# Turning three more chunks with VectorE and DRAM instead of TensorE, with the tokens of turned chunks in another order

## Chip, cores and metric

The kernel runs on one core of a Trainium2 chip. The metric is the device time of one execution in microseconds, as the median over runs; the profile is one further execution that the hardware profiler recorded. Engines are named as in the profile: PE is TensorE (PEld its weight loads), DVE is VectorE, ACT is ScalarE, POOL is GpSimd, SP is SyncE, which issues the DMAs here.

## What is computed

Two transformer layers over 2048 tokens of width 448, each an attention with 16 heads of width 28 that share one key and one value head, and a gated feed-forward block of width 1792. Both layers use the same weights.

```python
def _A_ref(x, wq, wk, wv, wo):
    q = heads(x @ wq)                 # 16 heads, width 28
    k, v = x @ wk, x @ wv             # one head for all
    p = softmax(einsum("bhqd,bkd->bhqk", q, k) * 28 ** -0.5)
    return concat(einsum("bhqk,bkd->bhqd", p, v)) @ wo

def _B_ref(x, w_gate, w_up, w_down):
    return (silu(x @ w_gate) * (x @ w_up)) @ w_down

x = A_x                               # (1, 2048, 448)
for layer in range(2):
    x = x + _A_ref(layernorm(x), wq, wk, wv, wo)
    x = x + _B_ref(layernorm(x), w_gate, w_up, w_down)
```

## The kernel before

All products are taken in a split form: each fp32 operand is a high part and a low part (`xh`, `xl`), and three products of parts are added in PSUM. The tokens stand in four chunks of 512. A normalized chunk has its tokens on the partitions and must be turned, so that its 448 features stand on the partitions, before PE can multiply it by weights. There are two ways of turning:

- `flip` (L248): sixteen 128×128 transposes by PE into PSUM; then ACT casts the high part (L254) and DVE subtracts for the low part (L255, L264).
- `turn_tile` (L268, L271): DVE transposes a tile of 128 tokens in 32×32 blocks into `tb`, four stores (SP) put the blocks into their places in a DRAM tensor `xt`, in runs of 32 tokens (128 bytes); `rows3` (L130, L132) loads the whole turned chunk into an `xn` tile with three DMAs, and `halved` makes the two parts of it (casts L278, L282).

Before the change DVE turns only chunks 0 to 2 of the attention's output, in both layers, while the scores and softmax of later chunks run; everything else is flipped by PE, 160 transposes in all.

The feed-forward block works in units. A unit is one hidden tile `n` of a group `gi` (groups of `FG` = 2 tiles) for one chunk `c`. On PE a unit is: a first half of 11 pairs of products into two banks; the down projection of the unit before, part one; a second half of 10 pairs. Ahead of the parts that write a bank again, `between` (L325) lets ACT copy one column of each bank to `seen`, and PE waits for these copies. Then ACT takes Silu (L922), DVE the product (L923), ACT the high part (L924) and DVE the low part (L927) of the hidden tile. Down products of the unit go into the next one. With a chunk's last unit the residual `xres` gets its sum (`accumulate`: DVE L826; ACT L829 and POOL L830).

In the last group of layer 0 the next attention starts already. When a chunk's sum is done, which is in the unit after its last, `hand_over(c)` computes the statistics and orders the rest: `self.soon` is a list of steps that count down by one at the end of each unit, and run at zero; `self.mid` holds steps in the middle of a unit; `a.plan[n, 0]` and `a.plan[n, 1]` hold steps ahead of and behind projection `n`. `project` takes the next of the 16 projections (four rows of query/key/value per chunk); each copies its bank to a `stage` tile (L523, L524), stores it to `qd` and `kt` (L525, L528), and for two rows of a chunk turns the values on DVE and copies them on POOL (L531, L534). `maxima` (L424) takes the column maxima of a chunk at projections 6, 10 and 14; those of chunk 0 need the four query rows of chunk 0 back from DRAM (`fetch`, L444, with casts by POOL, L446).

Before the change the last group goes like this, with units as (c, n): chunk 0's normalization (L230) is at the end of (1,1), its flips in the middle of (2,0), two projections at the end of (2,0); chunk 1's normalization is at the end of (2,1), its flips in the middle of (3,0), one projection at the end of (3,0); chunk 2 is normalized at the end of (3,1) and flipped before projection 7; chunk 3's flips come before projection 11.

The order of instructions on each engine is the order in which the program issues them (`manual_schedule`); each engine works in order, so an instruction that waits holds up all that stands behind it on its engine. Tiles are laid out in pools in order of allocation; a tile that lies over an older one waits for the older one's last use. In the scores phase the pool `at` holds the buffers `pt0`, `single0`, ... of the exponentials (L614 to L619) and, in `turns`, `tb`.

Of the kernel before, what the change touches and what calls it, by code (L numbers as in the profile page):

```python
# [8 lines left out]
F32 = mybir.dt.float32  # L9
F32R = mybir.dt.float32r  # L10
# [5 lines left out]
P = 128  # L16
# [39 lines left out]
def forward(  # L56
# [54 lines left out]
    def bank(cands, hold=False):  # L111

        for _ in cands:
            turn[cands] = (turn.get(cands, -1) + 1) % len(cands)
            b = cands[turn[cands]]
            if b not in live:
                if hold:
                    live.add(b)
                return b, banks[b]
        raise AssertionError("no bank")  # L120
# [82 lines left out]
    def xtile(pool, again=None):  # L203

        return (
            pool.tile([P, 4, 512], F32R, name="xh"),
            pool.tile([P, 3, 512], F32R, name="xl"),
            again,
        )

    def norm_steps(c, pool=pers, twice=True):

        got = {}
        cs = slice(4 * c, 4 * c + 4)

        def stat(t):
            nc.vector.bn_stats(stats[:, 4 * c + t, :], xres[:, 4 * c + t, :])
            nc.vector.bn_aggr(mv[:, 4 * c + t, :], stats[:, 4 * c + t, :])

        def scale():  # L220
            rstd = pers.tile([P, 4], F32, name="rstd", bufs=2)
            nc.gpsimd.tensor_scalar(rstd, mv[:, cs, 1], 1.0, EPS, ALU.mult, ALU.add)
            nc.gpsimd.tensor_tensor(rstd, rstd, halfn, ALU.pow)
            got["r"] = rstd

        def apply(t):
            if t == 0:
                got["x"] = pool.tile([P, 4, 512], F32, name="xn")
            o, i, r = got["x"][:, t, 0:D], xres[:, 4 * c + t, :], got["r"][:, t : t + 1]
            nc.vector.tensor_scalar(o, i, mv[:, 4 * c + t, 0:1], r, ALU.subtract, ALU.mult)  # L230
            if twice:
                nc.gpsimd.tensor_copy(got["x"][:, t, D:512], o[:, 384:D])

        fs = [lambda t=t: stat(t) for t in range(4)] + [scale]
        return fs + [lambda t=t: apply(t) for t in range(4)], got
# [7 lines left out]
    def flip(got, tiles, ks=range(4), place=None):  # L243

        for k in ks:
            pt = place if place is not None else bank(wide[-1])[1]
            for t in range(4):
                nc.tensor.transpose(pt[:, P * t : P * t + P], got["x"][:, t, P * k : P * k + P], ident)  # L248
            flipped(tiles, k, pt, nc.vector.tensor_copy if place is not None else nc.scalar.copy)
# [13 lines left out]
            high = xd[64:128, :]  # L263
        nc.vector.tensor_tensor(xh[64:128, k, :], pt[64:128, :], high, ALU.subtract)  # L264

    def turn_tile(got, tb, raw, t):

        nc.vector.transpose(tb[:, t, :], got["x"][:, t, 0:D])  # L268
        to = raw.rearrange("(b d) (t g w) -> t g d b w", d=32, g=4, w=32)
        for g in range(4):  # L270
            nc.sync.dma_start(to[t, g], tb[32 * g : 32 * g + 32, t, :].rearrange("d (b w) -> d b w", w=32))  # L271

    def halved(tiles, r, ks, copy, sub):

# [54 lines left out]
    class Attention:  # L329


        def __init__(self, layer):
            self.layer = layer
            self.X, self.norms, self.qd = {}, {}, {}
            self.done = 0
            self.order = [(c, m) for c in range(NC) for m in (TURN if c < NC - 1 else LAST)]
            self.seen = 0
            self.steps, self.places = [], []
            self.lent, self.plan = None, {}
            self.hi, self.rowsof, self.kt, self.when = {}, {}, {}, {}  # L340
            for c in range(NC):
                self.kt[c] = dram.tile([32, 512], F32, name=f"kt{layer}_{c}")
                self.at(4 * c + 4, lambda c=c: self.key_load(c))
                self.at(4 * c + 7, lambda c=c: self.key_split(c))
            for i in range(3):
                self.at(4 + 3 * i, lambda i=i: self.stack(i))
                self.at(6 + 3 * i, lambda i=i: self.parts(i))
                if not full:
                    self.at((9, 11, 13)[i], lambda i=i: self.rows(i))
            if not full:  # L350
                self.at(2, self.first_keys)
                self.at(3, self.diagonal)
            for i in range(len(GR) if full else 0):
                fs, place = self.max_steps(i)
                if i == 1:
                    fs[KC] = lambda f=fs[KC]: (f(), self.places[0]())
                self.steps += fs
                self.places.append(place)
# [49 lines left out]
        def parts(self, i):  # L408
            q = qts[i % 3]
            split(q[:, 0, :], q[:, 1, :], qraw)  # L410
# [95 lines left out]

        def q(self, c, m):
            cs = slice(512 * c, 512 * c + 512)
            held, po = bank((3, 4, 5) if self.seen > len(self.order) - 4 else wide[-1], True)
            ms = slice(P * m, P * m + P)  # L510
            wh, wl = self.w
            product_T(po, [wh[:, k, ms] for k in range(4)], [wl[:, k, ms] for k in range(4)], self.X[c])
            if not full and self.seen in (6, 10, 14):
                self.maxima(self.seen // 4 - 1)
            live.remove(held)
            if c not in self.qd:
                self.qd[c] = dram.tile([D, 512], F32, name=f"qd{self.layer}_{c}")
            raw = self.pool.tile([P, 512], F32, name="stage")
            if not full and (c or not self.layer):
                if self.seen % 2 == 0:  # L520
                    self.two = wpool.tile([P, 2, 512], F32R, tag="wgh", name="q2", bufs=FG + 1)
                self.hi[m] = self.two[0:112, self.seen % 2, :]
                nc.scalar.copy(self.hi[m], po[0:112, :])  # L523
            nc.scalar.copy(raw, po)  # L524
            nc.sync.dma_start(self.qd[c][112 * m : 112 * m + 112, :], raw[0:112, :])  # L525
            d0, n = 16 * (m % 2), 12 if m % 2 else 16
            if m > 1:
                nc.sync.dma_start(self.kt[c][d0 : d0 + n, :], raw[112 : 112 + n, :])  # L528
                return
            vt = wpool.tile([P, 512], F32R, tag="wgl", name="vt", bufs=FG + 1).bitcast(F32)[96:128, :]  # L530
            nc.vector.transpose(vt, po[96:128, :])  # L531
            vt = vt.rearrange("p (t u d) -> p u t d", t=4, u=4)
            for u in range(4):
                nc.gpsimd.tensor_copy(  # L534
                    vsb[32 * u : 32 * u + 32, 4 * c : 4 * c + 4, d0 : d0 + n], vt[:, u, :, 16 : 16 + n]
                )
# [17 lines left out]
        def scores(self, ff, xb):  # L554
            next(switch)
            inner = ExitStack()
            with tc.tile_pool(name=f"ow{self.layer}", bufs=1, side="right", reuse_waits="tile") as ow:
                wp = inner.enter_context(tc.tile_pool(name=f"at{self.layer}", bufs=1, reuse_waits="tile"))
                woh = ow.tile([P, NG, D], F32R, name="woh")
                wol = ow.tile([P, NG, D], F32R, name="wol")  # L560
                on, accs, pts = {}, {}, {}
# [140 lines left out]

                def turns(c, got):

                    at_ = {}

                    def one(t):
                        if t == 0:
                            at_["tb"] = wp.tile([P, 4, D], F32, name="tb")
                        turn_tile(got, at_["tb"], ff.raw[c], t)  # L710

                    return [lambda t=t: one(t) for t in range(4)]

# [68 lines left out]
    class FeedForward:  # L782
# [61 lines left out]
        def hand_over(self, c):  # L844

            a = self.nxt
            fs, got = norm_steps(c)
            for f in fs[:5]:
                f()
            a.pool = self.stage  # L850
            a.X[c] = xtile((xpool, self.x1p, self.xbp, self.xbp)[c])

            def ready():
                for f in fs[5:]:
                    f()
                if c > 1:
                    a.norms[c] = got

            if c == NC - 1:
                a.plan[8, 0] = [ready]  # L860
                return
            self.soon.append([1, ready])
            if c < 2:
                self.mid[len(groups) - 1, c + 2, 0] = [lambda ks=ks: flip(got, a.X[c], ks) for ks in ((0, 1), (2, 3))]
                self.soon.append([2, lambda: [a.project() for _ in range(2 - c)]])

        def fetch(self, c):

# [19 lines left out]
        def unit(self, gi, c, n):  # L888
# [30 lines left out]
            two = halves("h2")  # L919
            hh, hl = two[:, 0, :], two[:, 1, :]  # L920
            sg = pers.tile([P, 512], F32, name="sg")
            nc.scalar.activation(sg, pg[0], AF.Silu)  # L922
            nc.vector.tensor_tensor(sg, pg[1], sg, ALU.mult)  # L923
            nc.scalar.copy(hh, sg)  # L924
            for f in first[:2]:
                f()
# [144 lines left out]
```

## Time and profile before

| | us |
|---|---|
| median of 3 runs | 1992.53 |
| lowest, highest run | 1992.45, 1994.26 |
| the profiled execution | 1995.44 |
| its span | 1993.7 |

The span is the stretch of the profiled execution from its first to its last recorded instruction. TensorE's granted clock was 0.997 of full speed.

| engine | busy us | share of the span |
|---|---|---|
| PE | 1973.1 | 99% |
| ACT | 1276.1 | 64% |
| DVE | 782.7 | 39% |
| POOL | 559.9 | 28% |

How to read rows of the profile: a group's row has the source line, the engine, the operation, output and input by the program's names, the shape of both, the count, then busy time in us, the mean of one in ns, and the idle time of the engine just before such instructions with what ended it. A row of the timeline has the start and the length in us, the engine (SPq is SP's queue, PEld weight loads), the line, the operation, and in brackets the idle time before it and what ended that. A row of the windows has a stretch of time and its length, the busy time of PE, PEld, DVE, ACT and POOL, each with the number of instructions, then the granted clock, the busy share of the DMA engines and GB/s. A row of the chain has the start and the length of a piece and what it was.

### The profile page before, as it was taken

How to read it: one execution, taken by the hardware profiler on the slowest of the kernel's cores; microseconds unless marked ns; L12 is line 12 of the kernel's file. 1: busy time of each engine (PE TensorE's matmuls, PEld its weight loads, DVE VectorE, ACT ScalarE, POOL GpSimd, SP SyncE). 2: the span in 40 equal slices, each digit the busy share in tenths (PEclk: the TensorE clock that was granted, in tenths of full speed). 3: DMA queues.
4: the chain of work that ended last, by engine and by line, in shares of the span. 5: the costliest groups of instructions: out<-in, count | busy, mean ns of one | idle time of the engine just before them, and what ended most of it. 6: DMA issues, size and time to landing. Idle time of an engine off the chain costs nothing.

```text
span 1993.7 us, 43630 instructions
## 1 busy us (share of the span) xinstructions
PE 1973.1 (99%) x18517; PEld 1305.8 (65%) x18517; DVE 782.7 (39%) x1370; ACT 1276.1 (64%) x2140; POOL 559.9 (28%) x611
## 2 busy tenths in 40 slices
PE   8999999999999999999999999999999999999998
PEld 7544534445458999999884444444454689988886
DVE  6443343443534232322464444435444432222222
ACT  4799798997963333333348997979979433333332
POOL 4213123122214233333341221132231243233320
PEclk9999999999999999999999999999999999999999
DMA  5201011021120111100031010200212200011102
GB/s 156 61 23 33 17 30 44 17 51 32 39 62 22 31 32 31 32 18 25 22 95 40 26 30 12 62 12 22 51 32 62 53 17 27 21 31 32 32 1 76
DMA packets 126496, 75.50 MB, mean 38 GB/s; under 512 B 69688, under 2 KB 110008, under 8 KB 126296
## 3 DMA queue, kind: packets, MB, share of 16 engines
q1 hardware_dynamic: 124744, 71.46, 13.5%
q8 instruction: 146, 2.39, 0.5%
q10 hardware_dynamic: 1552, 1.20, 0.2%
q14 instruction: 54, 0.44, 0.1%
HBM read 54.01 MB, written 17.83 MB: 36 GB/s over the span
## 4 chain that ended last, share of the span: by engine, by line
PE 96%; DVE 1%; DMA 1%; ACT 1%; POOL 0%; issue 0%; ACTq 0%; SPq 0%; DVEq 0%; POOLq 0%
PE bank L318 40%; PE bank L651 25%; PE three L592 20%; PE bank L298 4%; PE bank L592 3%; PE three L577 2%; PE bank L577 2%; PE bank L248 1%; DMA wr<-in_A_wq_dram 0%; DMA qd<-stage 0%; DVE xn L230 0%; DMA xd<-xh 0%; DMA kt<-stage 0%; DVE xres L581 0%; PE bank L424 0%
## 5 line engine op out<-in xcount | busy, mean ns | idle before, releaser
L651 PE MATMUL bank<-pt,vsb 128*32 128x512 f32 x3072 | 491.9, 600 | 0.0
L651 PE MATMUL bank<-single,vsb 128*32 128x512 f32 x1024 | 488.6, 600 | 0.0
L592 PE MATMUL bank<-qstack,keys 32*128 32x512 f32 x1536 | 470.5, 424 | 2.2 <-DVE xres L581 1.7
L592 PE MATMUL three<-qstack,keys 32*128 32x512 f32 x4608 | 461.7, 425 | 3.6 <-ACT pt L615 2.4
L318 PE MATMUL bank<-xh,wgh 64*128 64x512 f32 x1728 | 446.4, 389 | 0.0
L592 PEld LDWEIGHTS three<-qstack,keys 32*128 32x128 f32 x4608 | 251.6, 183 | 297.0 <-ACT pt L615 187.6
L618 ACT ACTIVATE pt<-three 128x1536 f32<-128x1536 f32 x256 | 408.7, 1597 | 0.0
L615 ACT ACTIVATE pt<-three 128x1536 f32<-128x1536 f32 x256 | 405.3, 1583 | 2.6 <-DMA kt<-stage 2.6
L318 PE MATMUL bank<-xh,wgl 64*128 64x512 f32 x1404 | 368.5, 390 | 0.0
L318 PE MATMUL bank<-xl,wgh 64*128 64x512 f32 x1296 | 334.7, 389 | 0.0
L318 PE MATMUL bank<-wdh,h 64*128 64x448 f32 x1792 | 332.5, 364 | 1.5 <-ACT h L924 0.8
L923 DVE TENSOR_TENSOR sg<-bank,sg 128x512 f32<-128x512 f32 x112 | 77.5, 692 | 507.6 <-ACT sg L922 503.5
L318 PEld LDWEIGHTS bank<-xh,wgh 64*128 64x128 f32 x1728 | 263.0, 184 | 18.1 <-issue 1.6
L651 PEld LDWEIGHTS bank<-pt,vsb 128*32 128x32 f32 x3072 | 101.9, 109 | 261.2 <-issue 153.3
L830 POOL TENSOR_TENSOR xres<-stage,xres 128x448 f32<-128x448 f32 x108 | 127.2, 1197 | 498.3 <-ACT stage L829 498.1
L660 DVE TENSOR_TENSOR o<-bank,o 128x512 f32<-128x512 f32 x224 | 154.9, 692 | 277.7 <-PE bank L651 277.7
L617 DVE COPY single<-bank 128x512 f32<-128x512 f32 x256 | 177.0, 691 | 211.4 <-PE bank L592 205.0
L318 PEld LDWEIGHTS bank<-wdh,h 64*128 64x128 f32 x1792 | 244.5, 184 | 16.0 <-issue 2.3
L694 POOL TENSOR_TENSOR o<-o 128x512 f32<-128x512 f32 x32 | 41.3, 1290 | 740.2 <-DMA o<-rd 331.6
L592 PEld LDWEIGHTS bank<-qstack,keys 32*128 32x128 f32 x1536 | 243.8, 183 | 5.4 <-DVE xres L581 3.6
L325 ACT COPY seen<-bank 128x1 f32<-128x1 f32 x664 | 81.9, 163 | 255.0 <-PE bank L318 252.3
L614 ACT ACTIVATE single<-bank 128x512 f32<-128x512 f32 x256 | 187.8, 734 | 64.4 <-PE bank L592 64.4
(131 smaller groups left out, 2716.8 us busy)
## 6 DMA issues: line engine op xcount, KB each, us to landing
o<-rd SPq DMA_DIRECT2D x32, 256.0 KB
qd<-stage SPq DMA_DIRECT2D x32, 224.0 KB
qraw<-qd SPq DMA_DIRECT2D x128, 56.0 KB
wdr<-in_B_w_down_dram SPq DMA_DIRECT2D x28, 224.0 KB
xt<-tb SPq DMA_DIRECT2D x96, 56.0 KB
wr<-in_B_w_gate_dram SPq DMA_DIRECT2D x28, 192.0 KB
wr<-in_B_w_up_dram SPq DMA_DIRECT2D x28, 192.0 KB
xn<-xt SPq DMA_DIRECT2D x6, 768.0 KB
```

Of the source, the lines that this page charges most:

```text
L298: nc.tensor.matmul(po, a, b, start=(i == 0), stop=(i == len(seq) - 1))
L318: nc.tensor.matmul(po, a, b, start=start, stop=stop, skip_group_check=True)
L325: nc.scalar.copy(seen[:, i : i + 1], po[:, 0:1])
L577: nc.tensor.matmul(po[:, 0:D], a[:, g, ts_], b[:, g, :], start=(g + z == 0), stop=(g == NG - 1 and z == 2))
L592: nc.tensor.matmul(three[:, j, :] if j < 3 else one, k[js, kp, ks], q[js, part, :], start=(z == 0), stop=(z == 2), tile_position=(32 * j, 0),)
L614: es = [nc.scalar.activation(pt1, a, AF.Exp, scale=SCALE)]
L615: es.append(nc.scalar.activation(pt, threes[0], AF.Exp, scale=SCALE))
L617: copy = nc.vector.tensor_copy(pt1, b)
L618: es.append(nc.scalar.activation(pt, threes[1], AF.Exp, scale=SCALE))
L651: nc.tensor.matmul(to[32 * j : 32 * j + 32, :], vsb[:, n % NT, :], pts[n][j], start=(y == 0), stop=(y == 1), skip_group_check=True,)
L660: f = nc.vector.tensor_tensor(accs[i][:, 0, :], to, accs[i][:, 0, :], ALU.add)
L830: nc.gpsimd.tensor_tensor(r, s, r, ALU.add)
```

## The change

1. `turn_tile` no longer stores. It writes its transposed blocks so that `tb` holds, for each of four groups of 32 partitions, the whole chunk; a new `send` then stores the chunk with four DMAs, in runs of 128 tokens (512 bytes), behind the fourth transpose. The tokens of a turned chunk thereby stand in the order (g, t, w) instead of (t, g, w).
2. The readers put them back. `natural` and `in_order` are views in runs of 32: used by Silu and the product of all units of chunks 0 to 2 (84 of 112), by the copies of `q` for the turned chunks of layer 1's attention, and by the copies of the values on POOL.
3. Layer 1's attention input, chunks 0 to 2, goes the way of `turn_tile` too. `turn` (normalize, four transposes, four stores, load) is at the end of units (1,1), (2,1) and (3,1); `parts` (the casts and subtractions) is at the end of (2,0) for chunk 0, at the end of (3,0) for chunk 1, and behind projection 5 for chunk 2. Chunk 0's two projections move from the end of (2,0) to the end of (2,1); the one at the end of (3,0) stays. The 48 transposes of these chunks on PE go, and so does POOL's second copy of their normalized columns (L232).
4. In the scores phase `tb` is allocated once, first in its pool, instead of anew for each chunk behind the other buffers.

```diff
-    def turn_tile(got, tb, raw, t):
+    def turn_tile(got, tb, t):
 
-        nc.vector.transpose(tb[:, t, :], got["x"][:, t, 0:D])
-        to = raw.rearrange("(b d) (t g w) -> t g d b w", d=32, g=4, w=32)
+        nc.vector.transpose(tb[:, :, 32 * t : 32 * t + 32], got["x"][:, t, 0:D].rearrange("p (b w) -> p b w", w=32))
+
+    def send(tb, raw):
+
+        to = raw.rearrange("(b d) (g n) -> g d b n", d=32, g=4)
         for g in range(4):
-            nc.sync.dma_start(to[t, g], tb[32 * g : 32 * g + 32, t, :].rearrange("d (b w) -> d b w", w=32))
+            nc.sync.dma_start(to[g], tb[32 * g : 32 * g + 32])
+
+    def natural(po, squares):
+        ...
+        return po.rearrange("p (g t w) -> p t g w", g=4, w=32)
+
+    def in_order(a, squares):
+
+        return a.rearrange("p (t g w) -> p t g w", g=4, w=32) if squares else a
...
+            self.squares = (0, 1, 2) if layer else ()
...
-                nc.scalar.copy(self.hi[m], po[0:112, :])
-            nc.scalar.copy(raw, po)
+                nc.scalar.copy(in_order(self.hi[m], sq), natural(po[0:112, :], sq))
+            nc.scalar.copy(in_order(raw, sq), natural(po, sq))
...
-            vt = vt.rearrange("p (t u d) -> p u t d", t=4, u=4)
+            vt = vt.rearrange("p (u t d) -> p u t d" if sq else "p (t u d) -> p u t d", t=4, u=4)
...
                 wp = inner.enter_context(tc.tile_pool(name=f"at{self.layer}", bufs=1, reuse_waits="tile"))
+                tb = wp.tile([P, D // 32, P], F32, name="tb")
...
                     def one(t):
-                        if t == 0:
-                            at_["tb"] = wp.tile([P, 4, D], F32, name="tb")
-                        turn_tile(got, at_["tb"], ff.raw[c], t)
+                        turn_tile(got, tb, t)
+                        if t == 3:
+                            send(tb, ff.raw[c])
...
         def hand_over(self, c):
...
-            fs, got = norm_steps(c)
+            fs, got = norm_steps(c, twice=c == NC - 1)
             for f in fs[:5]:
                 f()
             a.pool = self.stage
-            a.X[c] = xtile((xpool, self.x1p, self.xbp, self.xbp)[c])
...
             if c == NC - 1:
+                a.X[c] = xtile(self.xbp)
                 a.plan[8, 0] = [ready]
                 return
-            self.soon.append([1, ready])
-            if c < 2:
-                self.mid[len(groups) - 1, c + 2, 0] = [lambda ks=ks: flip(got, a.X[c], ks) for ks in ((0, 1), (2, 3))]
-                self.soon.append([2, lambda: [a.project() for _ in range(2 - c)]])
+            raw = dram.tile([D, 512], F32, name=f"xt1_{c}")
+
+            def turn():
+                for f in fs[5:]:
+                    f()
+                pool = (xpool, self.x1p, self.xbp)
+                tb = pool[min(c + 1, 2)].tile([P, 4, 512], F32R, name="xh").bitcast(F32)
+                tb = tb.rearrange("p a (b n) -> p (a b) n", n=P)[:, 0 : D // 32, :]
+                for t in range(4):
+                    turn_tile(got, tb, t)
+                send(tb, raw)
+                a.X[c] = xtile(pool[c])
+                got["raw"] = pers.tile([P, 4, 512], F32, name="xn")
+                rows3(got["raw"], raw)
+
+            def parts():
+                halved(a.X[c], got["raw"], range(4), nc.scalar.copy, nc.vector.tensor_tensor)
+
+            self.soon.append([1, turn])
+            if c == 2:
+                a.plan[5, 1] = [parts]
+                return
+            self.soon.append([2, parts])
+            self.soon.append([3 - c, lambda: [a.project() for _ in range(2 - c)]])
...
-            nc.scalar.activation(sg, pg[0], AF.Silu)
-            nc.vector.tensor_tensor(sg, pg[1], sg, ALU.mult)
+            sq = c < NC - 1
+            nc.scalar.activation(in_order(sg, sq), natural(pg[0], sq), AF.Silu)
+            nc.vector.tensor_tensor(in_order(sg, sq), natural(pg[1], sq), in_order(sg, sq), ALU.mult)
```

More of the change, by code (lines that the diff above doesn't have):

```diff
@@ L264, in flipped @@
         nc.vector.tensor_tensor(xh[64:128, k, :], pt[64:128, :], high, ALU.subtract)
-    def turn_tile(got, tb, raw, t):
-        nc.vector.transpose(tb[:, t, :], got["x"][:, t, 0:D])
-        to = raw.rearrange("(b d) (t g w) -> t g d b w", d=32, g=4, w=32)
+    def turn_tile(got, tb, t):
+        nc.vector.transpose(tb[:, :, 32 * t : 32 * t + 32], got["x"][:, t, 0:D].rearrange("p (b w) -> p b w", w=32))
+    def send(tb, raw):
+        to = raw.rearrange("(b d) (g n) -> g d b n", d=32, g=4)
         for g in range(4):
-            nc.sync.dma_start(to[t, g], tb[32 * g : 32 * g + 32, t, :].rearrange("d (b w) -> d b w", w=32))
+            nc.sync.dma_start(to[g], tb[32 * g : 32 * g + 32])
+    def natural(po, squares):
+        if not squares:
+            return po
+        return po.rearrange("p (g t w) -> p t g w", g=4, w=32)
+    def in_order(a, squares):
+        return a.rearrange("p (t g w) -> p t g w", g=4, w=32) if squares else a
     def halved(tiles, r, ks, copy, sub):
@@ L508, in q @@
             cs = slice(512 * c, 512 * c + 512)
+            sq = c in self.squares
             held, po = bank((3, 4, 5) if self.seen > len(self.order) - 4 else wide[-1], True)
@@ L703, in turns @@
                 def turns(c, got):
-                    at_ = {}
                     def one(t):
-                        if t == 0:
-                            at_["tb"] = wp.tile([P, 4, D], F32, name="tb")
-                        turn_tile(got, at_["tb"], ff.raw[c], t)
+                        turn_tile(got, tb, t)
+                        if t == 3:
+                            send(tb, ff.raw[c])
                     return [lambda t=t: one(t) for t in range(4)]
@@ L855, in ready @@
                     f()
-                if c > 1:
-                    a.norms[c] = got
+                a.norms[c] = got
             if c == NC - 1:
+                a.X[c] = xtile(self.xbp)
                 a.plan[8, 0] = [ready]
                 return
-            self.soon.append([1, ready])
-            if c < 2:
-                self.mid[len(groups) - 1, c + 2, 0] = [lambda ks=ks: flip(got, a.X[c], ks) for ks in ((0, 1), (2, 3))]
-                self.soon.append([2, lambda: [a.project() for _ in range(2 - c)]])
+            raw = dram.tile([D, 512], F32, name=f"xt1_{c}")
[19 more added lines that the diff above has]
+            self.soon.append([3 - c, lambda: [a.project() for _ in range(2 - c)]])
         def fetch(self, c):
```

## Prediction

> **What bounds the kernel now.** I read the page's busy shares and its chain first. They say whether an engine that isn't the bound can matter.
>
> ```profile
> PE 1973.1 (99%) x18517; PEld 1305.8 (65%) x18517; DVE 782.7 (39%) x1370; ACT 1276.1 (64%) x2140; POOL 559.9 (28%) x611
> PE 96%; DVE 1%; DMA 1%; ACT 1%; POOL 0%; issue 0%; ACTq 0%; SPq 0%; DVEq 0%; POOLq 0%
> ```
>
> PE is busy 99% of the span and 96% of the chain. So work taken from PE is gained in full, and every microsecond in which PE waits for a new chain of DVE, DMA and ACT work is lost in full. The question is how much PE work goes and where PE would newly stand still. Call T(c,n) the start of the Silu of the last group's unit n of chunk c; the timeline of ScalarE between 940 and 1036 us has them:
>
> ```profile
> 960.20 0.60 ACT L922 ACTIVATE sg<-bank 128x512 f32<-128x512 f32 x1 [1.96 <-PE bank L318]
> 967.49 0.60 ACT L922 ACTIVATE sg<-bank 128x512 f32<-128x512 f32 x1 [2.15 <-PE bank L318]
> 977.71 0.60 ACT L922 ACTIVATE sg<-bank 128x512 f32<-128x512 f32 x1 [1.87 <-PE bank L318]
> 990.46 0.60 ACT L922 ACTIVATE sg<-bank 128x512 f32<-128x512 f32 x1 [1.97 <-PE bank L318]
> 1000.68 0.60 ACT L922 ACTIVATE sg<-bank 128x512 f32<-128x512 f32 x1 [1.87 <-PE bank L318]
> 1010.93 0.60 ACT L922 ACTIVATE sg<-bank 128x512 f32<-128x512 f32 x1 [1.97 <-PE bank L318]
> ```
>
> They are T(1,0), T(1,1), T(2,0), T(2,1), T(3,0), T(3,1). A unit takes 967.49 − 960.20 = 7.29 us. The two that hold sixteen transposes take 10.22 (967.49 to 977.71) and 10.22 (990.46 to 1000.68); the rest differ by projections.
>
> **What goes: transposes on PE.** Two chunks give 10.22 − 7.29 = 2.93 each. Chunk 2's sixteen stand in the chain by themselves.
>
> ```profile
> L248 PE MATMUL bank<-ident,xn 128*128 128x128 f32 x160 | 22.1, 279 | 1.7 <-DVE xn L230 1.2
> 1026.81 1.75 PE bank L248 x16
> ```
>
> That is 1.75, together 2 × 2.93 + 1.75 = 7.6 us. The group bounds it: 48 of 160 transposes of 22.1 us are 6.6.
>
> **What moves: the buffer tb, first in its pool.** It shifts the score buffers by its size. In layer 0 the first three-bank exponential then no longer lies over a stage buffer whose store is still under way:
>
> ```profile
> 71.27 1.45 ACT L615 ACTIVATE pt<-three 128x1536 f32<-128x1536 f32 x1 [2.57 <-DMA kt<-stage]
> 72.77 0.50 PE L592 MATMUL three<-qstack,keys 32*128 32x512 f32 x3 [2.42 <-ACT pt L615]
> ```
>
> ACT waits 2.57 and PE 2.42 for that store. Without it PE starts after the exponential; I take −2.6, bounds −2.4 and 0 (if another buffer waits). In layer 1 the wait changes places: `single` now lies over the stage buffer, where before DVE's copy waited.
>
> ```profile
> 1056.02 0.60 ACT L614 ACTIVATE single<-bank 128x512 f32<-128x512 f32 x1
> 1056.51 1.81 DMA kt<-stage
> 1058.46 0.69 DVE L617 COPY single<-bank 128x512 f32<-128x512 f32 x1 [3.85 <-DMA kt<-stage]
> ```
>
> The first exponential can't start at 1056.02 but after the earlier store's landing, between 0 and 1.8 us later; DVE's 3.85 goes. I take +1.0. Together −1.6, and with the transposes −9.2.
>
> **What is added: a round trip through DRAM.** For each of the three chunks DVE normalizes four tiles and transposes them, SP sends four stores and three loads, ACT casts four pieces. DVE's part has rows:
>
> ```profile
> 970.11 1.77 DVE L230 TENSOR_SCALAR xn<-xres,mv,rstd 128x448 f32<-128x448 f32 x4
> L268 DVE STREAM_TRANSPOSE tb<-xn 128x448 f32<-128x448 f32 x24 | 15.2, 635 | 0.0
> ```
>
> It starts 970.11 − 967.49 = 2.62 after T, so the tiles are turned at T + 2.62 + 1.77 + 4 × 0.635 = T + 6.95, off PE. Then comes R, from the first store's issue to the landing of the load. The scores phase has the same trip once, with the last tile's four stores:
>
> ```profile
> 552.22 2.12 SPq L271 DMA_DIRECT2D xt<-tb  x4
> 554.39 0.50 SPq L130 DMA_DIRECT2D xn<-xt  x1
> 554.93 2.24 SPq L132 DMA_DIRECT2D xn<-xt  x2
> 554.00:555.00 1.00, 1.00 (x16) 0.29 (x12) 0.53 (x1) 1.00 (x2) 0.00 (x0) 1.00 0.68 103
> 558.00:559.00 1.00, 1.00 (x13) 0.37 (x16) 0.69 (x1) 1.00 (x1) 0.00 (x0) 1.00 1.11 397
> 561.00:562.00 1.00, 1.00 (x16) 0.45 (x16) 0.23 (x1) 1.00 (x3) 0.00 (x0) 1.00 0.00 0
> ```
>
> The last column is GB/s: about 100 while the stores of 128-byte pieces drain, 397 in the load, nothing from 561. So the trip is over by 561, at most 8.8 after 552.22; I take R = 8.7 here, 6.5 of it from the load's issue on. After the change the four stores carry the whole chunk, 917 KB where these carry 229 KB, in pieces of 512 bytes. The nearest row for such pieces is
>
> ```profile
> 446.00:446.50 0.50, 0.50 (x8) 0.30 (x8) 0.18 (x1) 0.50 (x1) 0.00 (x0) 1.00 0.99 293
> ```
>
> At 293 GB/s the additional 688 KB take 2.3 us; some lies beside the 2.1 us of issue. So R is 8.7 (all hidden) to 11.1 (none), and I take 10.2, nearer the upper end since the load waits for the last store. The Trainium skill's page "DMA: Bandwidth & Descriptors", section "Anatomy of one DMA — SWDGE (gpsimd) path", gives 2.0 us and bytes over 436 GB/s for each transfer: an estimate of 4.1 for the stores and 4.1 for the load, R = 8.2, and by the sum below +0.6; the trace has 6.5 for the load, so here the row decides.
>
> Who waits for R? ACT is in order. The casts of chunk 0 are queued at the end of unit (2,0); behind them stand the `seen` copies, for which PE must wait before its second half of a unit.
>
> ```profile
> 575.67 1.80 ACT L278 CAST xh<-xn 128x512 fp32r<-128x512 f32 x3
> 577.22 0.77 ACT L282 CAST xh<-xn 128x512 fp32r<-128x512 f32 x1
> 618.11 0.38 ACT L325 COPY seen<-bank 128x1 f32<-128x1 f32 x2 [1.61 <-PE bank L318]
> 975.09 0.19 PEld L318 LDWEIGHTS bank<-xh,wgh 64*128 64x128 f32 x2 [0.17 <-issue]
> ```
>
> Casts (577.99 − 575.67, rounded up) and copies take 2.4 + 0.35. The second half starts 977.71 − 975.09 = 2.62 before a Silu, so PE wants it in unit (2,1) at T(1,1) + 2 × 7.29 − 2.62 = T + 11.96. It gets it at T + 6.95 + R + 2.75. **Chunk 0 loses R − 2.3 = 7.9 us.** All that hides the trip is one unit.
>
> Chunk 1 has more cover: the two projections moved to the end of (2,1) stand between, and unit (3,0). Its stores start at about T(2,1) + 8.0, behind the projections' own stores on SP; casts and copies add 3.3 (one more projection copy of 0.55); PE wants its second half in (3,1) at T(2,1) + 20.4 (1010.93 − 990.46 − 2.62 − 2.93, and the two moved projections, 990.46 − 977.71 − 7.29 = 5.46). **It loses R − 9.1 = 1.1**, nothing if R is under 9.1.
>
> Chunk 2's casts come late, but its stores and load stand on SP before the store of query rows 3 and the fetch that the column maxima need.
>
> ```profile
> 1013.54 1.78 DVE L230 TENSOR_SCALAR xn<-xres,mv,rstd 128x448 f32<-128x448 f32 x4
> 1016.02 2.07 SPq L444 DMA_DIRECT2D wrq<-qd  x4
> 1022.93 2.02 POOL L446 CAST q<-wrq 112x1024 fp32r<-112x1024 f32 x2
> 1025.88 0.93 PE bank L424 x4
> ```
>
> Stores leave at T(3,1) + 7.0; behind the load 0.3 for the row's store, 2.3 for the last fetch (0.5 issue, 1.8 landing as in the row of 1056.51), 1.0 for the second Pool cast: maxima at T + 10.6 + R, where they now start at 1025.88 − 1010.93 = T + 14.95. PE stands in the queue with the maxima in front. **It loses R − 4.35 = 5.85.** If the fetch overtakes the load, as little as nothing; the casts of chunk 2 are hidden behind this.
>
> **What is rewritten at no cost: the strided views.** In 84 of 112 units Silu and product read banks in runs of 32. No trace shows them so; a product over a repeated mask takes what a plain one takes:
>
> ```profile
> L394 DVE TENSOR_TENSOR kdiag<-few,mask 112x512 fp32r<-112x512 f32 x2 | 1.4, 692 | 0.1
> L923 DVE TENSOR_TENSOR sg<-bank,sg 128x512 f32<-128x512 f32 x112 | 77.5, 692 | 507.6 <-ACT sg L922 503.5
> 962.21 0.69 DVE L927 TENSOR_TENSOR h<-sg,h 128x512 fp32r<-128x512 f32 x1 [0.16 <-ACT h L924]
> 963.57 0.55 PE L318 MATMUL bank<-wdh,h 64*128 64x448 f32 x2
> ```
>
> And the last of a unit's chain ends at 962.90, 0.67 before PE's product at 963.57 wants it. Their cover is 0.67 us a unit; I take 0, with bounds 0 and, past the cover, 84 times the excess. The fewer stores in the scores phases (36 issues of 2.12 / 4 = 0.53 saved per layer) free SP, which nothing in the chain waits for: 0. Pool's second copy of the normalized columns goes, off the path: 0.
>
> **Sum.** −9.2 + 7.9 + 1.1 + 5.85 = +5.65 us. The profiled execution took 1995.44 (span 1993.7), so it would show 2001.1; it lies 2.9 over the median of 1992.53, against which the sum is **1998.2**. With R = 8.7 it is −9.2 + 6.4 + 0 + 4.35 = +1.6, with 11.1 it is −9.2 + 8.8 + 2.0 + 6.75 = +8.4. Zero lies at R = 7.9.
>
> The skill speaks against the change too: page "VectorE: DVE Perf Modes", section "Rules for kernel authors", advises TensorE for a 128×128 transpose that may land in PSUM. The price it avoids is the trip, whose terms above don't need it.
>
> **Rivals.** A measurement of this kernel can tell some 0.2%, 4.0 us.
> (1) Quick trip, faster side. If the stores drain while they are issued, the load follows at once and other transfers needn't stand behind it, R is 2.1 of issue + 1.8 of landing (the row of 1056.51) + 2.3 (917 KB at 397 GB/s) = 6.2, and chunk 2's fetch comes in time: −9.2 + 3.9 + 0 + 0 = −5.3, 1987.2. For it speaks the rate of 397; against it the 6.5 measured from the load's issue on. It decides below R = 7.9. 22%, of which 14 beyond 4 us.
> (2) Strided reads exceed the 0.67. At 0.80 extra a unit, 84 × 0.13 = 11 more: +16.7, 2009. The point of decision is 0.67; against it stands the 692 of L394. 9%.
> (3) The gain of layer 0 isn't there, because another shifted buffer waits as long, and layer 1 waits 1.8: +3.4 more, +9.0, 2001.5. 12%.
> (4) The turn doesn't get done as told: the transposes, now written to strided places, double to 1.27, which puts T + 6.95 at T + 9.5 and adds 2.5 to each of three trips: +13, 2005.6. 7%.
> The forecast has 50%: R of 8.7 to 11.1, 15 within 4 us and 35 above. So faster 14%, same 8 + 15 = 23%, slower 35 + 28 = 63%. Range: 1988.5 (half of the quick trips below it) to 2006.0 (over it the strided case and some of the doubled transposes); the forecast's own is 1994 to 2001.
>
> **What would show it.** In the timeline after: casts of L278's kind at the end of unit (2,0) that wait for a DMA of `xn`, followed by `seen` copies and a PE idle time of 7 to 9 us there; maxima late by 4 to 7 us with Pool's cast waiting on a DMA; no DMA wait ahead of L615 in layer 0; Silu at 601 ns and product at 692 as before. It is wrong if PE has no idle time over 3 us between 950 and 1060, or if Silu and product got longer.

## The result

| | before | after |
|---|---|---|
| median us | 1992.72 (5 runs, 1992.45 to 1996.15) | 2005.78 (5 runs, 2004.39 to 2009.36) |
| the profiled execution, us | 1995.44 | 2009.36 |
| its span, us | 1993.7 | 2007.6 |

The ratio is 1.0063, with a 95% interval of 1.0048 to 1.0077: 13 us slower, inside the range and on the side that was forecast, but over twice the forecast of 5.65, and only 0.2 us under the range's upper end of 2006.0.

### The profile after

Line numbers in rows are those of each run's own kernel. Both profiled executions lie some 3 us above their medians, so they are compared with each other.

The page's busy line, and then from the groups Silu and the product, DVE's transposes of part 3 and the transposes that PE has left (columns: busy us, mean ns, idle time before):

```profile
PE 1971.1 (98%) x18469; PEld 1306.5 (65%) x18469; DVE 789.6 (39%) x1382; ACT 1275.6 (64%) x2140; POOL 556.6 (28%) x599
```

```profile
L956 ACT ACTIVATE sg<-bank 128x512 f32<-128x512 f32 x112 | 67.3, 601 | 220.3 <-PE bank L331 219.3 <-PE bank L311 1.0
L957 DVE TENSOR_TENSOR sg<-bank,sg 128x512 f32<-128x512 f32 x112 | 77.5, 692 | 508.1 <-ACT sg L956 504.0 <-PE bank L311 4.1
L268 DVE STREAM_TRANSPOSE xh<-xn 128x448 f32<-128x448 f32 x12 | 6.7, 611 | 0.0
L248 PE MATMUL bank<-ident,xn 128*128 128x128 f32 x112 | 15.0, 277 | 1.9 <-DVE xn L230 1.5
```

Silu and the product take 601 and 692 ns, as before. 48 transposes are gone, which took 22.1 − 15.0 = 7.1 us of PE. But PE's busy time falls by only 2.0: something else made PE slower while it was busy. Where it stood still is in PE's timeline of the hand-over, one row for each of the long idle times (in brackets):

```profile
983.84 0.79 PE L331 MATMUL bank<-xh,wgh 64*128 64x512 f32 x2 [8.18 <-ACT seen L338]
1010.93 0.50 PE L331 MATMUL bank<-xh,wgh 64*128 64x512 f32 x2 [1.54 <-ACT seen L338]
1022.25 0.50 PE L311 MATMUL bank<-xh,wh 128*128 128x512 f32 x1 [1.50 <-DVE xres L840]
1037.35 1.22 PE L438 MATMUL bank<-q,kdiag 112*128 112x512 f32 x2 [6.84 <-POOL q L460]
```

The first two rows are the second halves of units (2,1) and (3,1), released by ACT's `seen` copies; the third is a bank that DVE emptied late, because chunk 2's normalization and four transposes stood ahead of its sums; the last is the first `maxima`, released by POOL's cast of the fetched rows. What ACT, SP and POOL waited for stands in their timelines:

```profile
969.97 3.03 SPq L274 DMA_DIRECT2D xt<-xh  x4
976.23 0.38 SPq L130 DMA_DIRECT2D xn<-xt  x1
981.49 1.66 ACT L291 CAST xh<-xn 128x512 fp32r<-128x512 f32 x3 [7.95 <-DMA xn<-xt]
983.58 0.53 ACT L338 COPY seen<-bank 128x1 f32<-128x1 f32 x6
1020.10 3.00 SPq L274 DMA_DIRECT2D xt<-xh  x4
1026.22 0.38 SPq L130 DMA_DIRECT2D xn<-xt  x1
1027.88 0.53 SPq L540 DMA_DIRECT2D qd<-stage  x1
1028.50 4.32 SPq L458 DMA_DIRECT2D wrq<-qd  x4
1034.30 3.00 POOL L460 CAST q<-wrq 112x1024 fp32r<-112x1024 f32 x2 [6.58 <-DMA wrq<-qd]
```

Chunk 0's casts wait 7.95 us for the load, and six `seen` copies come in a heap behind them: they had been held up for all that time. Chunk 2's stores and load run on SP from 1020.10, ahead of the query row's store (1027.88) and the fetch. The third view is the windows (stretch, its length, PE, PEld, DVE, ACT, POOL, granted clock, DMA share, GB/s):

```profile
984.00:986.00 2.00, 2.00 (x10) 1.61 (x12) 0.73 (x2) 0.11 (x2) 0.00 (x0) 0.50 0.00 0
986.00:988.00 2.00, 2.00 (x12) 1.51 (x12) 0.00 (x0) 0.00 (x0) 0.00 (x0) 0.50 0.00 0
988.00:990.00 2.00, 2.00 (x17) 1.50 (x14) 0.69 (x1) 0.73 (x2) 0.00 (x0) 0.78 0.00 0
990.00:992.00 2.00, 2.00 (x9) 1.66 (x10) 1.48 (x4) 0.49 (x1) 0.00 (x0) 1.00 0.00 0
1038.00:1040.00 2.00, 2.00 (x6) 1.61 (x5) 1.36 (x2) 0.00 (x0) 0.00 (x0) 0.50 0.47 177
1040.00:1042.00 2.00, 2.00 (x6) 1.55 (x5) 1.57 (x5) 0.00 (x0) 0.16 (x1) 0.50 0.14 47
1042.00:1044.00 2.00, 2.00 (x7) 1.55 (x7) 0.00 (x0) 0.70 (x2) 1.70 (x6) 0.62 0.41 125
```

Behind both long pauses PE is busy all the time at half clock, for about five and six microseconds. That loses (0.16 + 2 + 2) × 0.50 + 2 × 0.22 = 2.5 us behind the first (from 983.84), and some 3 behind the second (from 1037.35). The Trainium skill, page "TensorE: Matmul & The Clock Gate", section "Part 1: The HAM clock gate (the "warmup" mystery)", says that the array's clock is halved after an idle window of some 3.4 us and comes back after as long a busy one. The trace agrees in kind: the clock falls 3.0 and 2.8 us after PE stopped and comes back 5.1 and 6.2 us after it started again (the last section has these times). The forecast had left it out.

The two starts of scores, in ACT's timeline, and the clock of the first in the windows, two rows of before and two of after:

```profile
68.67 1.47 ACT L631 ACTIVATE pt<-three 128x1536 f32<-128x1536 f32 x1
1070.02 0.60 ACT L630 ACTIVATE single<-bank 128x512 f32<-128x512 f32 x1 [1.42 <-DMA kt<-stage]
```

```profile
74.00:76.00 2.00, 1.88 (x16) 0.73 (x20) 0.51 (x1) 2.00 (x4) 0.00 (x0) 0.64 0.26 94
76.00:78.00 2.00, 2.00 (x16) 0.39 (x8) 0.18 (x1) 2.00 (x3) 1.00 (x2) 0.50 0.19 39
```

```profile
74.00:76.00 2.00, 2.00 (x32) 1.08 (x24) 0.69 (x1) 2.00 (x4) 0.00 (x0) 1.00 0.30 104
76.00:78.00 2.00, 2.00 (x20) 0.42 (x16) 0.69 (x1) 2.00 (x3) 0.94 (x2) 1.00 0.16 33
```

The wait of 2.57 in layer 0 is gone, and with it a stretch of half clock that stood behind it in the kernel before. In layer 1 the first single exponential now waits for a store.

Added up between milestones of the two profiled executions (the time at which the same instruction starts): up to the first Silu of layer 0, −4.3 us; to T(1,1), +0.2; from T(1,1) to T(3,1), +6.7; from there to the second `maxima`, +9.75; from the third `maxima` to the sixty-fifth product of exponentials and values in layer 1, +1.7; the rest −0.2. Together +13.9, the difference of the spans.

### The profile page after: what moved, and what is told of

Read it like the earlier page. It is cut to its first block, busy times and chain, and to the rows that moved or that the text cites. A ratio compares the mean times of both kernels' runs of the same rounds, so it can differ in the third digit from the quotient of the medians.

```text
span 2007.6 us, 43472 instructions
## 1 busy us (share of the span) xinstructions
PE 1971.1 (98%) x18469; PEld 1306.5 (65%) x18469; DVE 789.6 (39%) x1382; ACT 1275.6 (64%) x2140; POOL 556.6 (28%) x599
## 4 chain that ended last, share of the span: by engine, by line
PE 49%; DMA 1%; DVE 0%; ACT 0%; SPq 0%; POOL 0%; issue 0%; ACTq 0%; DVEq 0%; POOLq 0%
PE bank L331 20%; PE bank L667 12%; PE three L608 10%; PE bank L311 2%; PE bank L608 1%; PE three L593 1%; PE bank L593 1%; DMA xn<-xt 1%; DMA xt<-xh 0%; DMA wrq<-qd 0%; PE bank L438 0%; PE bank L248 0%; SPq L274 0%; POOL q L460 0%; DMA xd<-xh 0%
```

## Experiments

Theory A: the loss is PE standing still for the round trip at the hand-over, and its half clock behind the pauses; all else happens at the two starts of scores and comes from the place of `tb`. The rivals are named with each run. The expectations count the layers from 1, so that their layer 2 is layer 1 of the text. Times are medians; the kernel before had 1993.0 beside the first four, 1992.17 beside the next three, 1992.41 beside the last.

### Flips kept

```diff
-            self.squares = (0, 1, 2) if layer else ()
+            self.squares = ()
...
# hand_over as in the kernel before
```

> Parts 1, 2 and 4 of the change without part 3: new order of tokens, four stores a chunk, strided views, tb first; layer 2's attention input is flipped by PE as before. Theory A (the loss is PE standing still for the round trip at the hand-over, and running at half clock behind each pause; everything else happens at the two starts of scores): layer 0's start gains 4.1 us, layer 1's loses 2.7, so 1.4 below the kernel before, about 1991.3; no PE pause over 2 us between 950 and 1050. Rival B (strided reads or the larger stores cost what the forecast lacked): slower than before by some 6 us, about 1999, with Silu over 601 ns or the product over 692 ns.

### tb first only

```diff
                 wp = inner.enter_context(tc.tile_pool(name=f"at{self.layer}", bufs=1, reuse_waits="tile"))
+                tb = wp.tile([P, 4, D], F32, name="tb")
...
-                        if t == 0:
-                            at_["tb"] = wp.tile([P, 4, D], F32, name="tb")
-                        turn_tile(got, at_["tb"], ff.raw[c], t)
+                        turn_tile(got, tb, ff.raw[c], t)
```

> The kernel before with tb allocated once and first in its pool, nothing else. Theory A: the place of tb alone makes both changes at the starts of scores, so the same 1.4 below the kernel before, about 1991.3, within 1 us of the run with flips kept; in layer 0 no DMA wait ahead of the first three-bank exponential and full clock from 66 us on. Rival: the gain of layer 0 comes from the fewer stores; then this run is at 1992.7 or above.

Measured: 1991.46 with flips kept (ratio 0.9992, interval 0.9983 to 1.0002) and 1991.55 with `tb` first only (0.9993, 0.9983 to 1.0002). Theory A had 1991.3 for both. The strided views in 84 units, the four larger stores and the order of tokens together make 0.1 us between these two medians, far inside either interval (1.9 us to each side). In the trace of `tb` first only the first three-bank exponential (65.57) waits for nothing and the clock is 1.00 from 66 to 80 us, so the place of `tb` alone brings the gain of layer 0, not the fewer stores. So the whole loss of the change lies in its part 3, and the parts that remain would, by the medians, be 1.5 faster than before, which the intervals do not tell from nothing. The first of these kernels shows what stands against the gain of layer 0, in the timelines of ACT and PE at layer 1's start and the windows behind it:

```profile
1053.95 0.60 ACT L630 ACTIVATE single<-bank 128x512 f32<-128x512 f32 x1 [2.22 <-DMA kt<-stage]
1054.60 1.20 PE L438 MATMUL bank<-q,kdiag 112*128 112x512 f32 x4 [1.85 <-ACT single L630]
```

```profile
1056.00:1058.00 2.00, 1.96 (x20) 1.10 (x24) 1.86 (x5) 2.00 (x3) 0.00 (x0) 0.60 0.17 56
1058.00:1060.00 2.00, 2.00 (x20) 0.59 (x16) 0.87 (x2) 2.00 (x3) 0.00 (x0) 0.55 0.30 100
```

The exponential waits for the store, PE waits 1.85 for it, and some 3.4 us of half clock follow (0.60 and 0.55 in four microseconds).

### Chunk 2 flipped

```diff
-            self.squares = (0, 1, 2) if layer else ()
+            self.squares = (0, 1) if layer else ()
...
+            if c == 2:
+                a.X[c] = xtile(self.xbp)
+                self.soon.append([1, ready])
+                return
             raw = dram.tile([D, 512], F32, name=f"xt1_{c}")
```

> The changed kernel with chunk 2 of layer 2's attention input flipped by PE as before; chunks 0 and 1 still go through DRAM. Theory A: the maxima of chunk 0 wait because chunk 2's stores and load stand before the query row's store and the fetch on SP; without them the 6.8 us pause ahead of the maxima, 2.8 us of half clock behind it and the 1.5 us wait for DVE go, and 1.75 us of transposes come back: about 9.4 below the changed kernel's 2005.8, near 1996.5. The pause of 8 us in unit (2,1) stays. Rival (the fetch is late for another reason, such as Pool): about 2004 to 2006, with the pause still there.

Measured: 1998.56 (1.0025, 1.0014 to 1.0036), 7.2 below the changed kernel where 9.4 were expected. The pause ahead of the maxima is gone; SP's and POOL's timelines show why, and PE's that the first pause stays:

```profile
1019.25 2.20 SPq L458 DMA_DIRECT2D wrq<-qd  x4
1026.23 2.03 POOL L460 CAST q<-wrq 112x1024 fp32r<-112x1024 f32 x2
985.13 0.80 PE L331 MATMUL bank<-xh,wgh 64*128 64x512 f32 x2 [8.26 <-ACT seen L338]
1594.15 0.50 PE L331 MATMUL bank<-xd,wgl 64*128 64x512 f32 x1 [1.82 <-DMA xd<-xh]
```

The fetch is issued in 2.2 us instead of 4.32, and POOL waits for no DMA. From T(3,1) to the second `maxima` the kernel takes 27.5 us, as the kernel before does, where the change takes 37.25: that stretch's loss is chunk 2's trip, wholly. Of the missing 2.2 us, 1.8 are in the last row: at the start of layer 1's feed-forward PE waits 1.82 us for a DMA of `xd`, where the changed kernel waits 0.22 and the three later runs with chunk 2 flipped 0.77 to 1.39. Why that DMA is late is open.

### PE kept busy in the pause

```diff
+    def idle_work():
+        spare = banks[[b for b in LOW if b not in live][0]]
+        for _ in range(50):
+            nc.tensor.transpose(spare[:, 0:P], ident, ident)
...
+            if c == 0:
+                self.mid[len(groups) - 1, 2, 1] = [lambda: None, idle_work]
```

> The changed kernel with 50 transposes of the identity into a free bank, whose result nothing reads, put into the pause of unit (2,1): about 7 us of PE work where PE stands still for 8.2. Theory A: the pause is what lowers PE's clock, so the granted clock stays at 1.0 from 976 to 990 and the kernel gets 2.5 us faster than the changed one, near 2003.3. Rival C (what PE lost behind the pause is not the clock's, or not the pause's doing): 2005.8 or more, with the same five microseconds at 0.50 behind the pause.

Measured: 2007.38 (1.0067, 1.005 to 1.0084), where 2003.3 was expected; its four runs (2005.18 to 2008.66) lie among the changed kernel's five. By the total this went as the rival says; by the windows of the place it went as theory A says:

```profile
976.00:978.00 2.00, 2.00 (x21) 2.00 (x20) 0.00 (x0) 0.00 (x0) 0.00 (x0) 1.00 1.02 397
984.00:986.00 2.00, 2.00 (x18) 1.49 (x15) 0.69 (x1) 1.17 (x2) 0.00 (x0) 1.00 0.00 0
1008.00:1010.00 2.00, 2.00 (x12) 1.58 (x10) 0.00 (x0) 0.00 (x0) 0.93 (x4) 0.53 0.14 41
```

and in PE's timeline, at units (2,1) and (3,1), and in SP's, at the fetch:

```profile
981.43 0.50 PE L331 MATMUL bank<-xh,wgh 64*128 64x512 f32 x2 [2.54 <-ACT seen L338]
1006.76 0.50 PE L331 MATMUL bank<-xh,wgh 64*128 64x512 f32 x2 [2.06 <-ACT seen L338]
1026.15 6.11 SPq L464 DMA_DIRECT2D wrq<-qd  x4
```

Of the wait in unit (2,1) 2.54 us are left, the clock stays at 1.00 behind it, and the stretch from T(1,1) to T(2,1) takes 23.03 instead of 25.10: 2.1 won. Chunk 1's pause is 2.06 instead of 1.54, with its trip no shorter (11.9 from the first store to the casts, 11.4 in the change), and this time some three microseconds of lowered clock follow; at T(3,1) 0.85 of the 2.1 is left. The maxima's pause, whose length SP and the DMA set, is 8.88 instead of 6.84, since SP issues the fetch in 6.11 us instead of 4.32; that eats more than the rest, and why it takes longer is open. So PE's standing still is what lowers the clock, which is shown here. That filling one pause makes the kernel faster is not: what was won in unit (2,1) was lost further on, and the two kernels' runs overlap.

### Casts one unit later

```diff
-            self.soon.append([2, parts])
-            self.soon.append([3 - c, lambda: [a.project() for _ in range(2 - c)]])
+            self.soon.append([3, parts])
+            if c == 0:
+                self.soon.append([4, lambda: [a.project() for _ in range(3)]])
```

> Chunk 2 flipped by PE, and the casts one unit later than in the change: chunk 0's at the end of (2,1), chunk 1's at the end of (3,1), the three projections of chunk 0 that come before the last unit all at the end of (3,0). Theory A: with the trip of 11.5 us that the changed kernel shows, chunk 0's second half is ready at T(1,1) + 6.95 + 11.5 + 2.75 = T + 21.2, PE wants it in unit (3,0) at T + 19.25, a pause of 2.0 in place of 8.2; chunk 1's trip is hidden by three projections; the transposes of two chunks (5.9) are gained, the starts of scores give 1.4: 5.3 below the kernel before, near 1987.7, up to 1.5 more if the pause of 2 lowers the clock. Rival (a pause of about 8 us stays wherever the casts stand, since ACT's order or the shared load buffer holds them): 1996 to 1999 as with chunk 2 flipped alone.

### tb first in layer 0 only

```diff
-                tb = wp.tile([P, D // 32, P], F32, name="tb")
+                tb = wp.tile([P, D // 32, P], F32, name="tb") if self.layer == 0 else None
...
+                if tb is None:
+                    tb = wp.tile([P, D // 32, P], F32, name="tb")
```

> Flips kept, tb first in its pool in layer 0 only; in layer 1 it is allocated behind the exponentials' buffers, where it lay before. Theory A: layer 1's start is as in the kernel before, without the wait of the first single exponential for a store, so the 4.1 of layer 0 stay whole: near 1988.9. Rival (the loss at layer 1's start comes from something else than the place of tb): 1991.4, as with tb first in both layers.

Measured with flips kept: 1988.24 (0.9977, 0.9968 to 0.9986), where 1988.9 was expected. It is 3.9 below the kernel before beside it, where the run with `tb` first in both layers was 1.5 below the one beside it: 2.4 more (the bare medians differ by 3.2, but were taken beside different runs of the kernel before). The next pair, taken together, differs by 2.5 in the same way: the place of `tb` in layer 1 is what costs there. This kernel is faster than the one before and the changed one.

### Both together

The two edits before this one in one kernel, with chunk 2 flipped.

> The kernel with later casts and chunk 2 flipped, and tb first in layer 0 only. Theory A: both gains add up, 5.3 and 2.7: 8.0 below the kernel before, near 1985. Rival (the pause that is left lowers the clock and eats the rest): 1988 to 1990.

Measured: 1995.46 for the later casts alone (1.0012, 1.0003 to 1.0021), 1992.93 with `tb` first in layer 0 only (1.0005, 0.9996 to 1.0014). Both missed by some 8. Chunk 0's pause fell to 1.0, where theory A had 2.0, but a new one of 3.4 stood in unit (3,1). Of the second kernel, first PE's row among the waits between 980 and 1010 us (us in total, times, the longest), then the timelines of ACT and SP:

```profile
PE bank L331 <- ACT seen L338: 4.4, 2, 3.4
```

```profile
999.47 0.58 ACT L539 COPY stage<-bank 128x512 f32<-128x512 f32 x1 [8.44 <-DMA kt<-stage]
986.26 3.00 SPq L274 DMA_DIRECT2D xt<-xh  x4
992.65 0.38 SPq L130 DMA_DIRECT2D xn<-xt  x1
994.25 0.58 SPq L540 DMA_DIRECT2D qd<-stage  x1
```

I had moved three projections behind chunk 1's `turn`. Their stores stood on SP behind the trip (986.26 to 994.25), there are two `stage` buffers, and so the third projection's copy waited 8.44 on ACT, with the `seen` copies behind it: the same wait in another coat.

### Two projections, the third behind the last unit

```diff
-            if c == 0:
-                self.soon.append([4, lambda: [a.project() for _ in range(3)]])
+            self.soon.append([4 - c, lambda: [a.project() for _ in range(2 - c)]])
```

> As the kernel with later casts and tb first in layer 0 only, but two projections at the end of (3,0) and the third at the end of (3,1) behind chunk 1's casts. In the run before this one the third projection's copy waited 8.4 us for a stage buffer whose store stood on SP behind chunk 1's stores and load; with two projections the two buffers suffice. Theory A: the pause of 3.4 us in (3,1) and the 1.7 us of half clock behind it go, chunk 0's pause of 1.0 stays: -4.1 (layer 0's start) - 5.9 (transposes) + 1.0 + up to 2 behind (3,1), so 5 to 9 below the kernel before, near 1985 and below the 1988.2 of the run with flips kept. Rival (the trip holds up what stands behind it on SP or ACT wherever it is put): 1988 or more, no better than flips.

Measured: 1984.39 (0.9961, 0.9947 to 0.9975), 8 us below the kernel before and the fastest of all. PE's only idle time over 0.4 us from 970 to 1020 is this one, in unit (3,0):

```profile
980.61 0.50 PE L331 MATMUL bank<-xh,wgh 64*128 64x512 f32 x2 [0.93 <-ACT seen L338]
```

The granted clock is 1.00 in all windows from 974 to 1016. Against flips kept with `tb` first in layer 0 the median is 3.9 lower; four of the five runs (1983.79 to 1984.54) lie below all eleven of that kernel (1986.84 to 1989.24), one (1987.24) among them. So turning chunks 0 and 1 through DRAM does pay; in the change it was the place of the casts, of chunk 2's trip and of `tb` in layer 1 that did not.

## Why the prediction was right, and where it was not

- **Transposes, −7.6.** Held: the group lost 7.1 us. With the trips hidden (the last run against flips kept with `tb` first in layer 0) two chunks gain 1988.24 − 1984.39 = 3.9, where 5.9 was the term. In the two profiled executions the stretch from T(1,0) to the second `single` exponential of layer 1 is 1052.91 − 953.22 = 99.69 with flips and 1047.52 − 952.84 = 94.68 without: 5.0, the term less the pause of 0.9 that is left. Of what is missing from that, 0.77 is PE's wait for the DMA of `xd` at 1575.27 in the last run; the other has none.
- **Chunk 0, R − 2.3 = 7.9.** 8.18, by the mechanism that was named: ACT in order, casts ahead of `seen`. R itself was mis-sized: 981.49 − 969.97 = 11.5 where 10.2 was taken and 11.1 was the bound. The rows taken for the trip belong to two chunks: the stores at 552.22 are chunk 2's, and the load at 554.39 is chunk 1's (L735, `ff.fetch(1)`), whose last stores were issued by 425.93. So that load waited for no store. The trip of the kernel before whose load does wait is chunk 0's:

```profile
296.21 2.11 SPq L271 DMA_DIRECT2D xt<-tb  x4
299.74 0.39 SPq L130 DMA_DIRECT2D xn<-xt  x1
```

Here the load leaves 3.53 after the first store, 1.4 later than the 2.17 in the rows taken, and the same sum would have given R = 10.1 to 12.5. In the change it leaves 976.23 − 969.97 = 6.3 after the first store: four stores of 229 KB take 3.03 to issue instead of 2.12, and SP waits for their landing. The load itself was quicker (5.3 to the casts, 6.5 taken). That the pause was nevertheless only 0.3 longer is luck: the stores left at T + 6.56 (6.95 taken), casts and copies took 2.35 (2.75 taken), and PE came at T + 12.25 (11.96 taken), 1.1 together.
- **Chunk 1, 1.1.** 1.54, with R = 1008.09 − 996.69 = 11.4, for which the same working gives 2.3. Casts and copies took 2.84 (3.3 taken) and PE came at T(2,1) + 20.9 (20.4 taken).
- **Chunk 2, 5.85.** 6.84, and 1.50 that was missed: DVE's turn stood ahead of the sums that empty a bank for the next projection. Past the load the fetch and its casts were also longer: POOL's two casts took 3.00, 2.02 in the row of before.
- **The step that failed: PE at full clock behind a pause.** The sum counted a pause by its length. Two pauses over 6 us lost another 2.5 and 3 at half clock, the largest single part of what the forecast lacked. The rows for it stood in the trace of before (0.64 and 0.50 from 74 to 78 us, behind layer 0's wait of 2.42), and I read that wait without looking at the clock behind it. For the same reason the gain at layer 0's start was 4.3 in the profiled executions instead of 2.6 (2.6 at the first three-bank exponential, 71.27 to 68.67, and 4.0 by 80 us, behind the stretch of half clock).
- **Layer 1's start, +1.0.** 1.7 in the profiled execution, and 2.4 and 2.5 in the two pairs of runs that differ only in it, each run against the kernel before beside it: the wait for the store was within its bounds (1.42), the lowered clock behind it was not in the sum.
- **Rivals.** The quick trip is refuted by R = 11.5. The strided views cost nothing: 601 and 692 ns, and 0.1 us between two kernels with and without them. The gain of layer 0 was there. The transposes into strided places take 611 ns, not 1270.
- **The range.** The median of 2005.78 lies in it by luck. Its upper end of 2006.0 was set for strided reads and doubled transposes, which the runs refute; the forecast's own mechanism had 1994 to 2001.
- **The two rules of the Trainium skill.** By the fit of the Trainium skill, page "DMA: Bandwidth & Descriptors", section "Anatomy of one DMA — SWDGE (gpsimd) path", R would have been an estimated 8.2. That fit is for transfers issued by GpSimd; these are issued by SP, and the trace has 11.5. The advice of the Trainium skill, page "VectorE: DVE Perf Modes", section "Rules for kernel authors", to take TensorE for a 128×128 transpose held for the change as it was. It did not hold for the last run, where the trip lies beside PE work.

Sum, against the forecast of +5.65 in the profiled execution's +13.9: half clock at the hand-over about +5.5 to 6, chunk 2's pauses +2.5, chunks 0 and 1 +0.7, layer 1 +0.7, layer 0 −1.7.

## What to carry to other kernels

Work taken from the bounding engine is worth its own time only if the detour lies beside other work from end to end: look at what stands behind each of its waiting instructions on every in-order queue, the DMA queue and a pool with two buffers included. A pause of PE can cost more than its length (2.5 and 3 us more here): read the granted clock in the windows behind it, and add half of the time that PE is busy while it is lowered. And where a buffer lies in its pool can be worth as much as the algorithm: about 4 us here, for the one line that makes `tb` first in layer 0.

## What the runs showed of the hardware that I had not expected

A pause needn't be long to lower the clock, and its length alone doesn't tell: with PE kept busy, the wait of 2.06 us in unit (3,1) did it, and the wait of 2.54 us in unit (2,1) of the same execution did not. When the clock changes is regular, though. These are the changed kernel's windows, cut where the clock changes:

```profile
978.65:988.89 10.24, 5.05 (x24) 4.02 (x26) 2.58 (x4) 2.99 (x11) 0.00 (x0) 0.50 0.27 84
988.89:1033.26 44.37, 38.40 (x245) 29.56 (x243) 24.46 (x49) 14.97 (x41) 9.42 (x16) 1.00 0.43 124
1033.26:1043.50 10.24, 6.15 (x15) 4.86 (x16) 7.07 (x10) 3.19 (x7) 4.45 (x7) 0.50 0.55 165
1043.50:1070.81 27.31, 25.63 (x137) 20.50 (x136) 13.12 (x24) 12.41 (x24) 16.61 (x36) 1.00 0.43 123
1070.81:1074.22 3.41, 3.41 (x20) 2.29 (x24) 1.47 (x3) 3.01 (x3) 0.00 (x0) 0.50 0.14 38
```

The stretches are 3, 13, 3, 8 and 1 times 3.41 us long: the clock changes only at points of a grid of 3.41 us, and so it is in the other traces. In the run with PE kept busy it is lowered from 1008.10 to 1011.51; counted back from there in steps of 3.41, the two waits fall into the grid like this:

```profile
977.38:980.79 3.41, 1.51 (x14) 1.27 (x12) 1.05 (x2) 1.70 (x4) 0.00 (x0) 1.00 0.46 121
1004.69:1008.10 3.41, 1.35 (x14) 1.12 (x14) 3.20 (x5) 2.34 (x10) 0.01 (x1) 1.00 0.18 53
```

The wait of 2.54 lies across a point of the grid, with 1.90 us of it ahead and 0.64 behind; the wait of 2.06 lies whole in one step, and the clock is lowered for the next step. So where a pause falls counts as well as how long it is. The grid isn't tied to the program: within its first 20 us the clock is lowered from 16.55 in the kernel before, from 11.41 with PE kept busy, and not at all in the last run. The Trainium skill, page "TensorE: Matmul & The Clock Gate", section "Part 1: The HAM clock gate (the "warmup" mystery)", has a window of 3.4 us that runs free of the kernel. The trace agrees on that, but not on a whole idle window: a step in which PE was busy for 1.35 us was enough. How much idle time in a step it takes stays open, since 1.90 us did not do it here, while 1.74 did in the run with casts one unit later (from 1011.00 to 1014.42).
